# A fourth PSUM bank and another order for the seven products of the first layer

## The chip, the cores and the metric

One core of one Trainium2 chip runs the whole program. The metric is device time in microseconds (us) of one execution; lower is better. Where several executions are shown, their median is the number that counts.

## The reference, cut to what matters

Three stages follow one another: attention over 2 batches of 8 heads, 768 positions, 64 wide, with a band of 96 local and 8 global keys; a soft mixture of 8 experts over the 1536 rows that come out of it; and a second feed-forward layer with a sigmoid gate.

```python
# attention, per batch and head
a = softmax(q @ k.T / 8 + bias, masked);  x = a @ v          # x: 1536 x 512 in all
# mixture: all experts see all rows, P is made doubly balanced in 8 rounds
P = exp(x @ w_gate - max)
for _ in range(8):
    P /= P.sum(1, keepdims=True) + 1e-09
    P /= P.sum(0, keepdims=True) + 1e-09
    P *= N / E
for e in range(8):
    h = np.maximum(x @ w1[e], 0.0)       # 512 -> 1024
    out += P[:, e:e + 1] * (h @ w2[e])   # 1024 -> 512
# second feed-forward layer on that output
h = x @ w_in                             # 512 -> 2048
g = h * (1.0 / (1.0 + np.exp(-1.702 * h)))
out = g @ w_out                          # 2048 -> 512
```

## The kernel before, in words

**Steps.** The hidden width of all layers is cut into units of 256: 32 units of the experts and 8 of the second feed-forward layer. `plan` (L531) lists 80 steps, each one unit for one batch of 768 rows. A step has two halves. `layer1` (L393) makes the hidden values of the unit; `layer2` (L472) multiplies them with the second weights and adds into the output. `mixture` (L600) runs layer 1 of step n and then layer 2 of step n-1, so that hidden values have one layer 1 of time to be finished. From unit 8 on a unit is used for batch 0 and then for batch 1 in two neighbouring steps; the second of the two also splits the weights of the next unit (L667, L673). In this document **call n** is the n-th layer 1, counted from 0 to 79; in the stage that matters most the odd calls are those that split weights.

**Layer 1.** Its matrix product is done as seven half-size products in the manner of Strassen and Winograd, named by their weight operand: A11, S2, A12, S3, S1, A22, S4 (`PRODUCTS`, L60). Each product is six matmuls of 384 columns, since every operand is split into a high and a low part (three passes over two chunks). The products accumulate in three PSUM banks x, y, z (tile names pl1x, pl1y, pl1z; pool `ps_m`, three buffers):

- x holds A11, which ScalarE copies into p1 (L452), and then A11 + A12, one finished quarter of the result.
- y holds S2, then S2 + S3, then S2 + S3 + A22. VectorE reads it each time: u2 = p1 + y after S2 (L454), u3 = p1 + y after S3 (L458), p1 = p1 + y after A22 (L460). All five of these adds are recorded at L403.
- z holds S1, then S1 + S4: u3 += z after S1 (L466), u2 += z after S4 (L463).

A product that adds into a bank must wait until VectorE or ScalarE has read what stands there. `put` (L408) turns a finished quarter into the high part hh and the low part hl. For the experts that is a ReLU: in phase 3 ScalarE writes hh and VectorE hl (L430); in phase 4 only the quarter in x goes that way, and the other three take a ReLU in place (L421), a copy (L422) and a subtraction on GpSimd (L425). For the second feed-forward layer it is a gate: sigmoid on ScalarE (L415), a multiply on VectorE (L418), the high part on ScalarE (L199) and the low part on GpSimd (L205). The part called `rest` (L449) is issued after the next product.

**Layer 2.** Six row tiles of 128 (groups 0 to 5 below), each six matmuls of 512 columns into one bank (L489, tile pl), which VectorE adds into the output (L500 for the experts, L498 and L506 elsewhere) or ScalarE copies.

**Banks.** `psum` (L519) hands out the eight banks: two of kind s, two of t, one of v, three of m. Phase 1 and 2 belong to the attention, which shares the machine with the first steps. Phase 3 begins when batch 1's attention is through (L1123); there layer 2 takes its banks in the order s, s, t, v. Phase 4 begins after the expert weights P are known and applied (L1136); there the order is s, s, t, t. The next layer-2 group that gets the same bank waits until the earlier one has been read.

**Order.** Instructions are issued by this Python code in program order on each engine (L1070); nothing reorders them. Other work is mixed in by `advance` (L607): after each product and each row tile it issues a piece of the side work that is due. In phase 3 that is the preparation of batch 1's operands (L276), the logits and the balancing rounds (L320, L345) and `combine` (L383); in phase 4 it is `doubles` (L221), which turns the float64 weights of the second feed-forward layer into float32 with nine VectorE instructions (L250 to L263) in five pieces per block.

Of the kernel before, what the change touches and what calls it, by code (L numbers as in the profile page):

```python
# [7 lines left out]
F32 = mybir.dt.float32  # L8
# [7 lines left out]
P = 128  # L16
# [13 lines left out]
def f(t):  # L30
    return t.bitcast(F32)
# [16 lines left out]
class Kernel:  # L48
# [8 lines left out]

    PRODUCTS = [  # L60
        ("A11", "B11", "x"),
        ("S2", "T2", "y"),
        ("A12", "B21", "x"),
        ("S3", "T3", "y"),
        ("S1", "T1", "z"),
        ("A22", "T4", "y"),
        ("S4", "B22", "z"),
    ]
# [199 lines left out]
    def operands_open(self, b, pool, tmp):  # L268

        x = {}  # L270
        for _, nm, _ in self.PRODUCTS:
            x[nm] = tuple(pool.tile([P, 2, self.HS], F32R, tag=f"{nm}{i}", name=f"{nm}{i}_{b}") for i in "hl")
# [120 lines left out]
    def layer1(self, v, u, b, first=False):  # L393

        nc = self.nc
        HS = self.HS
        ffn = self.units[u][2] is None
        hh = self.hp.tile([P, 2, self.S], F32R, tag="hh", name=f"hh_{v}_{b}")
        hl = self.hp.tile([P, 2, self.S], F32R, tag="hl", name=f"hl_{v}_{b}")
        p1 = self.up.tile([P, HS], F32, tag="p1", name=f"p1_{v}_{b}")  # L400
        u2 = self.up.tile([P, HS], F32, tag="u2", name=f"u2_{v}_{b}")
        u3 = self.up.tile([P, HS], F32, tag="u3", name=f"u3_{v}_{b}")
        add = lambda o, x, y: nc.vector.tensor_tensor(out=o, in0=x, in1=y, op=ALU.add)  # L403
        bank = {}

        late = []

        def put(c, fc, th):  # L408


            o = slice(th * HS, th * HS + HS)
            h, l = hh[:, fc, o], hl[:, fc, o]
            if ffn:
                sg = self.sgp.tile([P, HS], F32, tag="sg", name=f"sg_{v}_{b}_{fc}_{th}")
                nc.scalar.activation(sg, c, AF.Sigmoid, scale=1.702)  # L415

                def rest():
                    nc.vector.tensor_tensor(out=sg, in0=c, in1=sg, op=ALU.mult)  # L418
                    self.split(h, l, sg)
            elif self.phase == 4 and (fc or th):  # L420
                nc.scalar.activation(c, c, AF.Relu)  # L421
                nc.scalar.activation(h, c, AF.Copy)  # L422

                def rest():
                    nc.gpsimd.tensor_tensor(out=l, in0=c, in1=f(h), op=ALU.subtract)  # L425
            else:
                nc.scalar.activation(h, c, AF.Relu)  # L427

                def rest():
                    nc.vector.scalar_tensor_tensor(out=l, in0=c, scalar=0.0, in1=f(h), op0=ALU.max, op1=ALU.subtract)  # L430
            late.append(rest)

        seen = set()

        for an, bn, k in [self.PRODUCTS[n] for n in (0, 4, 2, 1, 3, 5, 6)] if first else self.PRODUCTS:
            ah, al = self.w1[v, an]
            bh, bl = self.xops[b][bn]
            new = k not in bank
            if new:
                bank[k] = self.ps_m.tile([P, HS], F32, tag="m", name=f"pl1{k}_{v}_{b}")  # L440
            ps = bank[k]
            for i, (x, y) in enumerate([(al, bh), (ah, bl), (ah, bh)]):
                for d in range(2):

                    nc.tensor.matmul(  # L445
                        ps, x[:, d, :], y[:, d, :], start=(new and i == 0 and d == 0), stop=(i == 2 and d == 1), skip_group_check=True
                    )
            while late:
                late.pop(0)()  # L449
            seen.add(an)  # L450
            if an == "A11":
                nc.scalar.activation(p1, ps, AF.Copy)  # L452
            elif an == "S2":
                add(u2, p1, ps)  # L454
            elif an == "A12":
                put(ps, 0, 0)
            elif an == "S3":
                add(u3, p1, ps)  # L458
            elif an == "A22":
                add(p1, p1, ps)  # L460
                put(p1, 1, 0)
            elif an == "S4":
                add(u2, u2, ps)  # L463
                put(u2, 0, 1)
            if an in ("S1", "S3") and {"S1", "S3"} <= seen:
                add(u3, u3, bank["z"])  # L466
                put(u3, 1, 1)
            yield an
        late.pop(0)()
        self.h[v, b] = hh, hl  # L470
# [48 lines left out]
    def psum(self, kind, shape, name):  # L519

        if kind == "2":
            self.turnover += 1
            kinds = {2: "m", 3: "sstv", 4: "sstt"}[self.phase]
            kind = kinds[self.turnover % len(kinds)]
        elif self.phase == 1:
            kind = {"s": "m", "p": "s"}.get(kind, kind)
        kind = "t" if kind == "p" else kind
        p = {"s": self.ps_s, "t": self.ps_t, "v": self.ps_v, "m": self.ps_m}[kind]
        return p.tile(shape, F32, tag=kind, name=name)
# [52 lines left out]
    def first_weights(self, eng):  # L582
# [5 lines left out]
        yield from self.sum_weights(0)  # L588
        for an, _, _ in self.PRODUCTS:
            self.split_w1(0, an, eng)  # L590
# [628 lines left out]
```

## Time and profile before

| | |
|---|---|
| median of 3 runs | 1487.26 us (1483.48 to 1487.72) |
| the profiled execution | 1492.43 us |
| its span, first to last instruction | 1490.4 us |
| TensorE (PE) busy | 1422.0 us, 95% of the span |
| VectorE (DVE) busy | 1135.6 us, 76% |
| GpSimd (POOL) busy | 860.1 us, 58% |
| ScalarE (ACT) busy | 644.5 us, 43% |
| mean granted TensorE clock | 0.986 of full speed |

The profile is of one execution; its times are in us from the first instruction. Busy time of PE is the time in which at least one matmul was under way; matmuls overlap, so a matmul's own duration (0.33 us for 384 columns) is longer than the distance to the next one (0.17 us). A group of the waits view gives for one engine and line how long it stood idle and whose work ended that wait. Shares over the whole span mix stages that have different limits, so the stages have to be looked at one by one: attention to 243.8 us, phase 3 (calls 6 to 13) to 403.4 us, then phase 4 with the conversion of weights (calls 14 to 61) to 1178.6 us, the change to the second feed-forward layer (calls 62 to 67) to 1291.9 us, and the rest.

### The profile page before, as it was taken

The page shows a single profiled execution, that of the slowest core. Times are in us where ns is not written, and L with a number is a line of the kernel's source. Part 1 is how long each engine was busy: PE and PEld are TensorE (multiplying, and loading weights), DVE is VectorE, ACT ScalarE, POOL GpSimd, SP SyncE. Part 2 cuts the span into 40 slices and gives each one's busy share as a digit, 9 for nine tenths or more (in the row PEclk, how much of TensorE's full clock was granted, in tenths as well). Part 3 has the DMA queues.
Part 4 walks back from the last instruction along what each step waited for, and adds up shares of the span by engine and source line. Part 5 has one row for each costly group of instructions (what it writes and reads, how often), then busy time and mean ns, then how long its engine had stood idle before and what let it go on. Part 6 is the DMA issues. An engine that isn't in the chain of part 4 may idle for free.

```text
span 1490.4 us, 21158 instructions
## 1 busy us (share of the span) xinstructions
PE 1422.0 (95%) x7295; PEld 1244.4 (83%) x7295; DVE 1135.6 (76%) x2199; ACT 644.5 (43%) x1511; POOL 860.1 (58%) x1003
## 2 busy tenths in 40 slices
PE   7899998999899999999999999999999988999999
PEld 5567887788888888898888888888888877899897
DVE  7987887467578888888888888788887576555655
ACT  5676767243443333333333333333333456534332
POOL 3645555657674555554555545455555686756652
PEclk9989999999999999999999999999999999999999
DMA  5322210111221222222121212112121111101002
GB/s 147 73 61 60 73 46 29 57 57 57 75 88 62 66 73 72 71 64 68 60 75 64 82 60 72 60 61 75 61 85 47 48 38 34 52 29 43 29 1 85
DMA packets 99348, 91.66 MB, mean 61 GB/s; under 512 B 42912, under 2 KB 76704, under 8 KB 99232
## 3 DMA queue, kind: packets, MB, share of 16 engines
q1 hardware_dynamic: 99232, 90.22, 19.2%
q8 instruction: 60, 0.98, 0.3%
q14 instruction: 56, 0.46, 0.1%
HBM read 78.66 MB, written 11.53 MB: 61 GB/s over the span
## 4 chain that ended last, share of the span: by engine, by line
PE 80%; DVE 13%; issue 3%; ACT 3%; POOL 2%; POOLq 0%; DVEq 0%; ACTq 0%
PE pl L489 41%; PE pl1y L445 14%; PE pl1z L445 10%; PE pl1x L445 8%; PE pv L928 2%; DVE u L403 2%; PE s L850 1%; DVE acc L500 1%; PE pt L887 1%; DVE a L876 1%; POOL w2l L205 1%; DVE acc L285 1%; DVE a L863 1%; DVE al L908 1%; DVE hl L430 1%
## 5 line engine op out<-in xcount | busy, mean ns | idle before, releaser
L489 PE MATMUL pl<-w2h,hl 128*128 128x512 f32 x960 | 300.9, 394 | 6.9 <-DVE acc L500 4.3
L489 PE MATMUL pl<-w2l,hh 128*128 128x512 f32 x960 | 297.2, 391 | 0.0
L489 PE MATMUL pl<-w2h,hh 128*128 128x512 f32 x960 | 297.1, 391 | 0.0
L500 DVE SCALAR_TENSOR_TENSOR acc<-pl,pr,acc 128x512 f32<-128x512 f32 x312 | 230.2, 746 | 74.5 <-PE pl L489 71.9
L205 POOL TENSOR_TENSOR w2l<-r,w2h 128x512 fp32r<-128x512 f32 x100 | 131.5, 1336 | 196.7 <-ACT w2h L199 178.1
L489 PEld LDWEIGHTS pl<-w2l,hh 128*128 128x128 f32 x960 | 180.5, 188 | 39.3
L489 PEld LDWEIGHTS pl<-w2h,hh 128*128 128x128 f32 x960 | 180.4, 188 | 38.8
L489 PEld LDWEIGHTS pl<-w2h,hl 128*128 128x128 f32 x960 | 176.8, 188 | 39.8 <-DVE acc L500 5.7
L425 POOL TENSOR_TENSOR hl<-u,hh 128x384 fp32r<-128x384 f32 x100 | 105.8, 1058 | 135.1 <-ACT hh L422 134.5
L199 ACT ACTIVATE w2h<-r 128x512 fp32r<-128x512 f32 x98 | 56.6, 624 | 207.6 <-PE pl L489 174.3
L403 DVE TENSOR_TENSOR u<-p,pl1y 128x384 f32<-128x384 f32 x160 | 87.8, 549 | 64.7 <-PE pl1y L445 52.5
L452 ACT ACTIVATE p<-pl1x 128x384 f32<-128x384 f32 x80 | 39.2, 490 | 182.2 <-PE pl1x L445 167.6
L403 DVE TENSOR_TENSOR u<-u,pl1z 128x384 f32<-128x384 f32 x160 | 88.1, 551 | 36.2 <-PE pl1z L445 33.7
L421 ACT ACTIVATE u<-u 128x384 f32<-128x384 f32 x100 | 52.1, 521 | 123.6 <-DVE u L403 123.1
L205 POOL TENSOR_TENSOR hl<-sg,hh 128x384 fp32r<-128x384 f32 x64 | 66.0, 1031 | 58.1 <-ACT hh L199 56.7
L205 POOL TENSOR_TENSOR S3l<-s,S3h 128x256 fp32r<-128x256 f32 x50 | 40.5, 810 | 99.4 <-ACT S3h L199 99.2
L192 POOL TENSOR_TENSOR s<-r 128x256 f32<-128x256 f32 x100 | 78.2, 782 | 0.0
L506 DVE TENSOR_TENSOR acc<-pl,acc 128x512 f32<-128x512 f32 x84 | 54.3, 682 | 19.9 <-PE pl L489 19.8
L866 ACT ACTIVATE a<-a,m 128x288 f32<-128x288 f32 (+2 forms) x96 | 48.1, 502 | 43.0 <-DVE m L863 43.0
L445 PE MATMUL pl1y<-T3h,S3l 128*128 128x384 f32 x160 | 44.4, 358 | 23.0 <-DVE u L403 22.9
L427 ACT ACTIVATE hh<-pl1x 128x384 fp32r<-128x384 f32 x64 | 31.4, 491 | 79.5 <-PE pl1x L445 79.4
L205 POOL TENSOR_TENSOR A22l<-r,A22h 128x256 fp32r<-128x256 f32 x50 | 44.0, 880 | 22.6 <-ACT A22h L199 22.3
(259 smaller groups left out, 3489.6 us busy)
## 6 DMA issues: line engine op xcount, KB each, us to landing
r<-in_moe_w_dram SPq DMA_DIRECT2D x82, 512.0 KB, 3.6
r<-d SPq DMA_DIRECT2D x18, 512.0 KB, 3.7
d<-in_moe_w_in_dram SPq DMA_DIRECT2D x32, 256.0 KB, 2.8
d<-cx SPq DMA_DIRECT2D x64, 128.0 KB, 1.7
d<-in_moe_w_out_dram SPq DMA_DIRECT2D x32, 256.0 KB, 3.0
out_dram<-acc SPq DMA_DIRECT2D x12, 256.0 KB, 2.1
k<-in_k_dram SPq DMA_DIRECT2D x28, 96.0 KB, 2.3
q<-in_q_dram SPq DMA_DIRECT2D x28, 96.0 KB, 2.5
```

Source lines behind the costliest of these rows:

```text
L192: nc.gpsimd.tensor_tensor(out=o, in0=x, in1=y, op=op)
L199: nc.scalar.activation(hi, x, AF.Copy)
L205: e.tensor_tensor(out=lo, in0=x, in1=f(hi), op=ALU.subtract)
L403: add = lambda o, x, y: nc.vector.tensor_tensor(out=o, in0=x, in1=y, op=ALU.add)
L421: nc.scalar.activation(c, c, AF.Relu)
L425: nc.gpsimd.tensor_tensor(out=l, in0=c, in1=f(h), op=ALU.subtract)
L445: nc.tensor.matmul(ps, x[:, d, :], y[:, d, :], start=(new and i == 0 and d == 0), stop=(i == 2 and d == 1), skip_group_check=True)
L452: nc.scalar.activation(p1, ps, AF.Copy)
L489: nc.tensor.matmul(ps, x[:, c, ts_], y, start=(i == 0 and c == 0), stop=(i == 2 and c == 1))
L500: nc.vector.scalar_tensor_tensor(out=acc, in0=ps, scalar=self.pr[:, tt, e : e + 1], in1=acc, op0=ALU.mult, op1=ALU.add)
L506: nc.vector.tensor_tensor(out=acc, in0=ps, in1=acc, op=ALU.add)
L866: nc.scalar.activation(s, s, AF.Exp, bias=m, scale=-1.0, accum_out=rs[:, j : j + 1])
```

## The change

From phase 3 on layer 1 uses a table of its own, `WIDE`: the product S3 gets a fourth bank w (pool `ps_v`, tile pl1w), S3 and S1 stand ahead of A12, and A22 starts the bank y anew where it added to S2 + S3 before. The five adds become a chain: u2 = p1 + y, u3 = u2 + w, p1 = u3 + z, then u3 = u3 + y after A22 and u2 = u2 + z after S4. The quarters become finished in the order (1,1), (0,0), (1,0), (0,1), where it was (0,0), (1,1), (1,0), (0,1). In phase 3 layer 2 rotates over s, s, t, since w takes the bank of kind v. Calls 0 to 5 keep the old table, calls 6 to 79 take the new one.

```diff
--- before.py
+++ after.py
     PRODUCTS = [
         ("A11", "B11", "x"),
         ("S2", "T2", "y"),
         ("A12", "B21", "x"),
         ("S3", "T3", "y"),
         ("S1", "T1", "z"),
+        ("A22", "T4", "y"),
+        ("S4", "B22", "z"),
+    ]
+    WIDE = [
+        ("A11", "B11", "x"),
+        ("S2", "T2", "y"),
+        ("S3", "T3", "w"),
+        ("S1", "T1", "z"),
+        ("A12", "B21", "x"),
         ("A22", "T4", "y"),
         ("S4", "B22", "z"),
     ]
@@ -432,12 +442,16 @@
         seen = set()
 
-        for an, bn, k in [self.PRODUCTS[n] for n in (0, 4, 2, 1, 3, 5, 6)] if first else self.PRODUCTS:
+        wide = self.phase >= 3
+        order = self.WIDE if wide else self.PRODUCTS
+
+        for an, bn, k in [order[n] for n in (0, 4, 2, 1, 3, 5, 6)] if first else order:
             ah, al = self.w1[v, an]
             bh, bl = self.xops[b][bn]
-            new = k not in bank
-            if new:
-                bank[k] = self.ps_m.tile([P, HS], F32, tag="m", name=f"pl1{k}_{v}_{b}")
+            new = k not in bank or wide and an == "A22"
+            if k not in bank:
+                p, tag = (self.ps_v, "v") if k == "w" else (self.ps_m, "m")
+                bank[k] = p.tile([P, HS], F32, tag=tag, name=f"pl1{k}_{v}_{b}")
             ps = bank[k]
@@ -454,15 +468,24 @@
                 add(u2, p1, ps)
             elif an == "A12":
                 put(ps, 0, 0)
+            elif an == "S4":
+                add(u2, u2, ps)
+                put(u2, 0, 1)
+            elif wide:
+                if an == "S3":
+                    add(u3, u2, ps)
+                elif an == "S1":
+                    add(p1, u3, ps)
+                    put(p1, 1, 1)
+                elif an == "A22":
+                    add(u3, u3, ps)
+                    put(u3, 1, 0)
             elif an == "S3":
                 add(u3, p1, ps)
             elif an == "A22":
                 add(p1, p1, ps)
                 put(p1, 1, 0)
-            elif an == "S4":
-                add(u2, u2, ps)
-                put(u2, 0, 1)
-            if an in ("S1", "S3") and {"S1", "S3"} <= seen:
+            if not wide and an in ("S1", "S3") and {"S1", "S3"} <= seen:
                 add(u3, u3, bank["z"])
                 put(u3, 1, 1)
             yield an
@@ -520,7 +543,7 @@
-            kinds = {2: "m", 3: "sstv", 4: "sstt"}[self.phase]
+            kinds = {2: "m", 3: "sst", 4: "sstt"}[self.phase]
```

TensorE in call 17 (unit 16, batch 1; pl1x to pl1w are the banks, h and l the high and low parts), between the product S2 and the product A22, before:

```order
L445 MATMUL pl1x_16_1_25453<-B21h_1_23376,A12l_16_25171 128x384 x2
L445 MATMUL pl1x_16_1_25453<-B21l_1_23377,A12h_16_25170 128x384 x2
L445 MATMUL pl1x_16_1_25453<-B21h_1_23376,A12h_16_25170 128x384 x2
L445 MATMUL pl1y_16_1_25463<-T3h_1_23378,S3l_16_25185 128x384 x2
L445 MATMUL pl1y_16_1_25463<-T3l_1_23379,S3h_16_25184 128x384 x2
L445 MATMUL pl1y_16_1_25463<-T3h_1_23378,S3h_16_25184 128x384 x2
L445 MATMUL pl1z_16_1_25507<-T1h_1_23380,S1l_16_25201 128x384 x2
L445 MATMUL pl1z_16_1_25507<-T1l_1_23381,S1h_16_25200 128x384 x2
L445 MATMUL pl1z_16_1_25507<-T1h_1_23380,S1h_16_25200 128x384 x2
```

and with the change:

```order
L459 MATMUL pl1w_16_1_25567<-T3h_1_23457,S3l_16_25262 128x384 x2
L459 MATMUL pl1w_16_1_25567<-T3l_1_23458,S3h_16_25261 128x384 x2
L459 MATMUL pl1w_16_1_25567<-T3h_1_23457,S3h_16_25261 128x384 x2
L459 MATMUL pl1z_16_1_25579<-T1h_1_23459,S1l_16_25274 128x384 x2
L459 MATMUL pl1z_16_1_25579<-T1l_1_23460,S1h_16_25273 128x384 x2
L459 MATMUL pl1z_16_1_25579<-T1h_1_23459,S1h_16_25273 128x384 x2
L459 MATMUL pl1x_16_1_25543<-B21h_1_23455,A12l_16_25290 128x384 x2
L459 MATMUL pl1x_16_1_25543<-B21l_1_23456,A12h_16_25289 128x384 x2
L459 MATMUL pl1x_16_1_25543<-B21h_1_23455,A12h_16_25289 128x384 x2
```

A12 moved behind S3 and S1, and S3 writes a bank of its own; A11 and S2 ahead of these rows, A22 and S4 behind them stand where they stood.

VectorE in the same call (cx, cy, cz and d belong to the conversion of weights, hl is the low part of a finished quarter), from the last piece of conversion ahead of the first add to the last add, before:

```order
L261 TENSOR_SCALAR cy_3_25390<-d_2_25279 128x256
L403 TENSOR_TENSOR u2_16_1_25451<-p1_16_1_25450,pl1y_16_1_25463 128x384
L263 SCALAR_TENSOR_TENSOR cx_3_25389<-cy_3_25390,cx_3_25389 128x256
L430 SCALAR_TENSOR_TENSOR hl_16_1_25449<-pl1x_16_1_25453,hh_16_1_25448 128x384
L403 TENSOR_TENSOR u3_16_1_25452<-p1_16_1_25450,pl1y_16_1_25463 128x384
L250 TENSOR_SCALAR cx_4_25502<-d_3_25387 128x256
L251 TENSOR_SCALAR cy_4_25503<-d_3_25387 128x256
L403 TENSOR_TENSOR u3_16_1_25452<-u3_16_1_25452,pl1z_16_1_25507 128x384
L403 TENSOR_TENSOR p1_16_1_25450<-p1_16_1_25450,pl1y_16_1_25463 128x384
L253 TENSOR_TENSOR cx_4_25502<-cx_4_25502,cy_4_25503 128x256
L254 TENSOR_SCALAR cy_4_25503<-cx_4_25502 128x256
L403 TENSOR_TENSOR u2_16_1_25451<-u2_16_1_25451,pl1z_16_1_25507 128x384
```

and with the change (line numbers are those of the changed file; L413 is the add, L440 the low part of the quarter in x, L260 to L273 the conversion):

```order
L271 TENSOR_SCALAR cy_3_25480<-d_2_25368 128x256
L413 TENSOR_TENSOR u2_16_1_25541<-p1_16_1_25540,pl1y_16_1_25553 128x384
L273 SCALAR_TENSOR_TENSOR cx_3_25479<-cy_3_25480,cx_3_25479 128x256
L413 TENSOR_TENSOR u3_16_1_25542<-u2_16_1_25541,pl1w_16_1_25567 128x384
L413 TENSOR_TENSOR p1_16_1_25540<-u3_16_1_25542,pl1z_16_1_25579 128x384
L260 TENSOR_SCALAR cx_4_25595<-d_3_25477 128x256
L261 TENSOR_SCALAR cy_4_25596<-d_3_25477 128x256
L440 SCALAR_TENSOR_TENSOR hl_16_1_25539<-pl1x_16_1_25543,hh_16_1_25538 128x384
L413 TENSOR_TENSOR u3_16_1_25542<-u3_16_1_25542,pl1y_16_1_25553 128x384
L263 TENSOR_TENSOR cx_4_25595<-cx_4_25595,cy_4_25596 128x256
L264 TENSOR_SCALAR cy_4_25596<-cx_4_25595 128x256
L413 TENSOR_TENSOR u2_16_1_25541<-u2_16_1_25541,pl1z_16_1_25579 128x384
```

The number of rows is the same. The second and third add moved ahead of the low part of x, and the read of y after S3 is gone.

## Rows read from the trace of the kernel before

**Rows 1.** The page, busy time of TensorE with its share of the span.

```profile
PE 1422.0 (95%) x7295; PEld 1244.4 (83%) x7295; DVE 1135.6 (76%) x2199; ACT 644.5 (43%) x1511; POOL 860.1 (58%) x1003
```

**Rows 2.** Windows by stage: length, busy PE, PEld, DVE, ACT, POOL, clock, DMA.

```profile
243.80:403.40 159.60, 149.82 (x733) 127.27 (x732) 104.57 (x200) 65.51 (x147) 108.10 (x121) 0.98 0.17 57
403.40:1178.60 775.20, 755.67 (x3745) 674.68 (x3744) 643.87 (x1152) 276.93 (x613) 428.31 (x471) 1.00 0.21 68
```

**Rows 3.** Waits of TensorE, 403.4 to 1178.6 and 1178.6 to 1291.9: total, times, longest.

```profile
PE pl1y L445 <- DVE u L403: 18.0, 22, 2.4
PE pl1x L445 <- ACT p L452: 0.9, 1, 0.9
...
PE pl1y L445 <- DVE u L403: 1.3, 1, 1.3
```

**Rows 4.** Timeline of TensorE (start, length): first product of calls 14, 24, 25, 62.

```profile
403.41 0.51 PE L445 MATMUL pl1x<-B11h,A11l 128*128 128x384 f32 x2
...
565.08 0.51 PE L445 MATMUL pl1x<-B11h,A11l 128*128 128x384 f32 x2
...
580.59 0.51 PE L445 MATMUL pl1x<-B11h,A11l 128*128 128x384 f32 x2
...
1178.64 0.51 PE L445 MATMUL pl1x<-B11h,A11l 128*128 128x384 f32 x2
```

**Rows 5.** Timeline of TensorE in call 17: first product, and S3 with its wait.

```profile
452.05 0.51 PE L445 MATMUL pl1x<-B11h,A11l 128*128 128x384 f32 x2
...
456.17 0.61 PE L445 MATMUL pl1y<-T3h,S3l 128*128 128x384 f32 x2 [0.80 <-DVE u L403]
```

**Rows 6.** Timeline of VectorE in the same call.

```profile
452.92 1.43 DVE L259 TENSOR_TENSOR cx<-cx,cz 128x256 f32<-128x256 f32 x1
454.28 1.37 DVE L261 TENSOR_SCALAR cy<-d 128x256 int32<-128x256 int32 x1
455.57 0.54 DVE L403 TENSOR_TENSOR u<-p,pl1y 128x384 f32<-128x384 f32 x1
```

**Rows 7.** Timeline of GpSimd in the same call.

```profile
452.79 2.71 POOL L205 TENSOR_TENSOR w2l<-r,w2h 128x512 fp32r<-128x512 f32 x2 [5.91 <-ACT w2h L199]
```

**Rows 8.** One line's instructions, L259 and L403: count, shortest/median/longest in ns.

```profile
L259 DVE TENSOR_TENSOR cx<-cx,cz x64: 405/419/1433, 430.3 to 1143.0; 128x256 f32<-128x256 f32 x64
...
L403 DVE TENSOR_TENSOR u<-p,pl1y x160: 535/553/556, 113.3 to 1467.3; 128x384 f32<-128x384 f32 x160
```

**Rows 9.** Timeline of call 6 (first product at 252.05): VectorE, then S4 on TensorE.

```profile
256.59 2.58 DVE L285 TENSOR_TENSOR tmp<-xf,tmp 128x768 f32<-128x768 f32 x1
...
262.28 0.98 PE L445 MATMUL pl1z<-B22h,S4l 128*128 128x384 f32 x2 [0.72 <-DVE u L403]
```

**Rows 10.** Timeline around the layer 2 at 360.76: reads of groups 0, 2 to 5; group 3; S3 of call 12.

```profile
365.25 0.68 DVE L498 TENSOR_TENSOR accx<-pl,accx 128x512 f32<-128x512 f32 x1
...
372.35 2.47 DVE L498 TENSOR_TENSOR accx<-pl,accx 128x512 f32<-128x512 f32 x4
...
364.88 0.62 PE L489 MATMUL pl<-w2h,hl 128*128 128x512 f32 x2
...
375.43 0.59 PE L445 MATMUL pl1y<-T3h,S3l 128*128 128x384 f32 x2 [3.15 <-DVE u L403]
```

**Rows 11.** Timeline of call 78 (gate): TensorE's A11 and next layer 2, then VectorE.

```profile
1447.37 0.51 PE L445 MATMUL pl1x<-B11h,A11l 128*128 128x384 f32 x2
...
1454.70 0.63 PE L489 MATMUL pl<-w2h,hl 128*128 128x512 f32 x2
...
1452.81 0.56 DVE L403 TENSOR_TENSOR u<-u,pl1z 128x384 f32<-128x384 f32 x1 [0.48 <-PE pl1z L445]
1454.02 0.56 DVE L418 TENSOR_TENSOR sg<-u,sg 128x384 f32<-128x384 f32 x1 [0.65 <-ACT sg L415]
...
1455.69 0.96 DVE L418 TENSOR_TENSOR sg<-p,sg 128x384 f32<-128x384 f32 x1 [0.65 <-ACT sg L415]
...
1458.64 1.87 DVE L506 TENSOR_TENSOR acc<-pl,acc 128x512 f32<-128x512 f32 x3
```

## The prediction, made before the change was run

> **What bounds the kernel now.** I read the page first. TensorE is busy for 95% of the span [rows 1], so only two things can shorten the run: less matmul work, or fewer moments in which TensorE waits. The change removes no matmul, so the waits are all there is to win. The windows by stage [rows 2] say where they lie: from 403.4 to 1178.6 us TensorE works 755.7 of 775.2 us and VectorE 643.9 of 775.2, so neither is idle for long. The waits of TensorE in that stage [rows 3] are nearly all of one kind: 18.0 us in 22 waits, the longest 2.4 us, in which a product that goes into bank y waits for an add that reads y. The waits view does not show all of the loss, so I also take the distance between first and last call there. Calls 14 and 62 begin 775.23 us apart [rows 4], with 48 calls and 48 layers 2 between them. Call 24, which has no wait, takes 15.51 us up to call 25, layer 2 included [rows 4]. 48 x 15.51 = 744.5, so 30.7 us are lost in this stage: the listed waits and the slow start after each.
>
> Call 17 shows how one arises. Product S3 begins at 456.17 after a wait of 0.80 us [rows 5]. The add u2 that it waits for ran from 455.57 to 456.11, behind two instructions of the weight conversion that took 1.43 and 1.37 us [rows 6]. The first of these kinds takes 0.42 us in the median [rows 8]; here GpSimd was splitting second weights for 2.71 us at the same time [rows 7], which it does at the start of each odd call. So VectorE is late by 1 to 2 us, and between S2 and S3 stands only one product, some 1.04 us (seven products take 7.3 us), to cover it.
>
> **Term 1, calls 14 to 61.** S3 and S1 now write banks that nobody has to read first. The read of y must be done by A22, which stands three products behind S2 instead of S3's one: 2 x 1.04 = 2.1 us more cover. The longest wait was 2.4 us, so 0.3 us of it is left, and nothing of a wait of 0.8. The copy of x by ScalarE gets the same cover, so its 0.9 us goes too [rows 3]. What is late next is the read of z: S4 waits for the third add. By the order on VectorE that add follows u2 with at most a piece of conversion and u3 between. In call 17: u2 ends 456.11, conversion 0.42, u3 0.55, third add 0.55, so 457.6, that is 5.6 us after the call began at 452.05; S4's place is 6 x 1.04 = 6.3 us after it. No wait, by 0.7 us. A further blocked instruction of 1.4 us would bring one, so I leave a tenth: gain 27.6 us, bounds 0 and 30.7.
>
> **Term 2, calls 62 to 67.** One wait for u2 of 1.3 us [rows 3] and its restart: gain 1.5, bounds 0 and 3.
>
> **Term 3, phase 3.** Two places. In call 6 a subtraction of 2.58 us for batch 1's operands holds VectorE from 256.59 to 259.17, and S4 begins only at 262.28 [rows 9]. In the new order u3 and the third add follow that subtraction directly: 259.17 + 0.55 + 0.55 = 260.3, so S4 comes 2.0 us sooner. The pair of matmuls there took 0.98 us instead of some 0.51: TensorE ran at the lower of its two clock levels after standing idle; if that goes too, up to 3 us more. The price is paid in the layer 2 at 360.76. With banks s, s, t instead of s, s, t, v its group 3 takes the bank of group 0 and its group 5 that of group 2. Group 0 is read until 365.93, while group 3 now begins at 364.88; groups 2 to 5 are read from 372.35 in 0.62 us each [rows 10], and group 5 has its place at 364.88 + 2 x 1.36 = 367.6. So TensorE would stand until 373.0, 5.4 us late, and the wait of 3.15 us at S3 in call 12 that follows is then gone, since VectorE has caught up: net loss 2.2 us, up to 5 if the clock falls. The sum of both places: 0, bounds -5 and +5.
>
> **Term 4, the gates, calls 64 to 79.** TensorE has no wait to lose there, and something can be lost. The quarters pass one after another through add, sigmoid, multiply and copy, VectorE and ScalarE waiting for each other, and VectorE reads no group of layer 2 before the last multiply. In call 78 the chain starts with the add at 1452.81 and the first read of layer 2 begins at 1458.64, that is 11.27 us after the call's start at 1447.37 [rows 11]. In the new order S1 is finished one product (1.04 us) sooner, but four quarters instead of three hang in the chain; one more link costs 1455.69 - 1454.02 = 1.67 us. So that read begins 0.6 us later, at 11.9, and ends at 12.5. Group 4, which takes that bank again, has its place at 7.33 + 4 x 1.365 = 12.8 (1454.70 - 1447.37 = 7.33). 0.3 us remain. In the eight odd calls GpSimd splits weights in between, and a part of that will show: loss 2 us in all, bounds 0 and 29 (16 calls, a second link of 1.67 and half of one blocked instruction in each).
>
> Added and removed instructions: none; the adds, copies and DMAs are the same in number, and POOL's and SP's queues keep their rows but for the place of the split of S3, which now needs to be ready third. It is made a whole layer 2 (8.2 us) ahead.
>
> **Sum.** -27.6 - 1.5 + 0 + 2 = -27.1 us. Against the profiled execution 1492.43 that is 1465.3; the median of the three runs is 1487.26, 5.2 us lower, which gives 1460 for what is measured.
>
> The rule that speaks against the change stands in the Trainium skill, SBUF — State Buffer, "Who interferes with whom": a VectorE instruction with two SBUF inputs and a GpSimd instruction that reads SBUF lock each other out for a whole instruction, and only a VectorE instruction with at most one SBUF input is free of it. The trace agrees: the conversion goes from 0.42 to 1.43 us, while the adds, which read one input from PSUM, never take over 0.556 us [rows 8]. By that rule the lost time of VectorE is not removed by any order of the products, only handed on; rival A is what it would do.
>
> **Rivals.**
> A. VectorE stays late and TensorE meets it elsewhere. For: VectorE is busy for 83% of the stage [rows 2]; and in the new order the low part of the quarter in x stands behind a ReLU chain on ScalarE, so VectorE stands still where it had work. Against: it is idle for 131 us of the stage, 2.7 us per call, and TensorE's loss is only 0.64 us per call. If half of term 1 came back at S4 or in the banks of layer 2: 1460 + 13.8 = 1474.
> B. More than forecast: all of term 1, term 2 and the low-clock stretch of call 6, without the loss in phase 3: 30.7 + 1.5 + 5 = 37, so 1450.
> C. The change does not do what it says for the time: S4 takes over S3's wait one for one, because the third add comes as late after S1 as u2 came after S2. For: both are reads by the same late engine. Against: two products instead of one stand between S1 and S4. Time 1484 to 1489.
> D. Slower: the chain of the gates (term 4). Its point: the first read must end 0.3 us later than I have it before TensorE waits at all, and every further us costs 16 us. To eat up the 29 us of terms 1 and 2 it must be late by 0.3 + 29 / 16 = 2.1 us, a second extra link and a blocked multiply in every call: then 1488, and 1493 at 2.4. Against: in call 78 the multiply of 0.96 us is already the blocked kind [rows 11].
>
> **How the numbers follow.** A measurement of this kernel can tell about 0.3%, 4.5 us, from no change. Forecast (a gain of 19 to 35 us) 0.65; A 0.14; B 0.08; C 0.07; D 0.06. Faster is the forecast, A and B: 0.87; same is C: 0.07; slower is D: 0.06. The range takes in the forecast with the bounds of term 3 and A: 1449 to 1476.
>
> **What would show it.** Right: the waits of pl1y for u2 between calls 14 and 61 fall from 18.0 us to under 3, the 48 calls with their layers 2 take about 747 us instead of 775, and a new wait of layer 2 for VectorE of some 5 us stands near 365 us in place of the 3.15 us at S3. Wrong: waits of pl1z for the adds of more than 10 us (A, C), waits of layer 2 for VectorE in the last 200 us (D), or a distance of calls above 15.5 us with no wait in it.

## The result and the profile after

| | kernel before | changed |
|---|---|---|
| median, runs on one chip | 1487.49 us (1483.48 to 1489.29, 4 runs) | 1464.34 us (1460.04 to 1465.24, 4 runs) |
| ratio, 95% interval | | 0.9842 (0.9814 to 0.9870) |
| profiled execution, its span | 1492.43, 1490.4 us | 1460.04, 1457.7 us |

The change is faster by 23 us, 1.6%; forecast were 1460 us and a range of 1449 to 1476. The page of the changed kernel, the line that answers to [rows 1]:

```profile
PE 1404.6 (96%) x7295; PEld 1238.7 (85%) x7295; DVE 1116.5 (77%) x2199; ACT 642.1 (44%) x1511; POOL 860.1 (59%) x1003
```

Every engine has as many instructions as before. TensorE is 17.4 us less busy with the same matmuls: 9.0 us less in calls 14 to 61 (746.7 instead of 755.7), and 6.0 us less before call 0 (74.6 instead of 80.6), where both kernels run the same code. In calls 14 to 61 part of this belongs to the waits: a pair of matmuls behind a stand, a moment in which TensorE waits, counts as busy for longer (0.61 us instead of 0.51, [rows 5]).

The windows by stage of the changed kernel (columns as in [rows 2]: length, busy PE, PEld, DVE, ACT, POOL, clock, DMA), calls 14 to 61, then calls 6 to 13 (the first line of [rows 2] begins earlier, at the start of phase 3):

```profile
398.50:1146.10 747.60, 746.66 (x3745) 674.79 (x3744) 629.45 (x1152) 277.26 (x613) 429.41 (x471) 1.00 0.22 70
245.50:398.50 153.00, 140.73 (x696) 119.70 (x696) 97.83 (x194) 58.33 (x134) 101.20 (x116) 0.99 0.17 56
```

In the stage of calls 14 to 61 VectorE does its 1152 instructions in 629 us, 14 us less than before, but in 27.6 us less time, and TensorE is idle for 0.9 us of 747.6. Its waits there, which answer to [rows 3] (waited for: total, times, longest), and the first products of calls 14 and 62, which answer to [rows 4]:

```profile
PE pl1z L459 <- DVE p L413: 0.4, 2, 0.3
PE pl1y L459 <- DVE u L413: 0.3, 1, 0.3
```

```profile
398.53 0.51 PE L459 MATMUL pl1x<-B11h,A11l 128*128 128x384 f32 x2
...
1146.11 0.51 PE L459 MATMUL pl1x<-B11h,A11l 128*128 128x384 f32 x2
```

The 48 calls with their layers 2 take 1146.11 - 398.53 = 747.58 us, where they took 775.23.

One profile against one profile says little of the stages that the change does not touch, so both kernels were profiled once more (runs e7 and e8 below). From the first products of calls 0, 6, 14, 62, 68 and the spans:

| us | before | before again | changed | changed again |
|---|---|---|---|---|
| start to call 0 | 98.5 | 94.3 | 90.6 | 90.7 |
| calls 0 to 5 | 153.5 | 154.8 | 154.9 | 154.9 |
| calls 6 to 13 (phase 3) | 151.4 | 151.4 | 153.0 | 153.0 |
| calls 14 to 61 | 775.2 | 773.4 | 747.6 | 747.6 |
| calls 62 to 67 | 113.2 | 112.3 | 113.1 | 115.8 |
| call 68 to the end | 198.5 | 198.6 | 198.5 | 198.6 |
| span | 1490.4 | 1484.9 | 1457.7 | 1460.5 |

The first pair differs by 32.7 us, the second by 24.4, the medians by 23. What the first pair has too much lies for the most part before call 0, where both kernels run the same code. Another 1.6 us of it lie in call 47 of the kernel before: behind its longest stand (2.36 us at S3) TensorE was granted the lower of its two clock levels (0.50 from 940.8 to 944.1), and the call took 19.72 us. In the second profile the same call, at the full clock, took 18.14.

Call 17 of the changed kernel shows how the gain comes about (VectorE, then GpSimd, then TensorE's S3 and S4):

```profile
445.92 1.45 DVE L269 TENSOR_TENSOR cx<-cx,cz 128x256 f32<-128x256 f32 x1
447.28 1.38 DVE L271 TENSOR_SCALAR cy<-d 128x256 int32<-128x256 int32 x1
448.59 0.54 DVE L413 TENSOR_TENSOR u<-p,pl1y 128x384 f32<-128x384 f32 x1
...
450.11 0.55 DVE L413 TENSOR_TENSOR p<-u,pl1z 128x384 f32<-128x384 f32 x1
```

```profile
445.78 2.73 POOL L215 TENSOR_TENSOR w2l<-r,w2h 128x512 fp32r<-128x512 f32 x2 [4.73 <-ACT w2h L209]
```

```profile
447.15 0.51 PE L459 MATMUL pl1w<-T3h,S3l 128*128 128x384 f32 x2
...
451.31 0.51 PE L459 MATMUL pl1z<-B22h,S4l 128*128 128x384 f32 x2
```

VectorE is held up exactly as before: 1.45 and 1.38 us for the two pieces of conversion, against 1.43 and 1.37 [rows 6], beside the same split on GpSimd. u2 begins at 448.59, 3.54 us after the call's start; before it was 3.52. But S3, which waited 0.80 us for it [rows 5], now begins at its place at 447.15, 1.44 us ahead of u2. The third add ends at 450.66 and S4 has its place at 451.31: 0.65 us to spare, where the prediction had 0.7. Not every odd call has so much. In seven of the 24 S4 begins 0.05 us after the third add ends, so it waited for it, in five of them by too little to be listed (call 19 is shown at e9).

### The profile page after: what moved, and what is told of

Same layout as the page of the kernel before. It is cut to its first block, busy times and chain, and to the rows that moved or that the text cites. A ratio compares the mean times of both kernels' runs of the same rounds, so it can differ in the third digit from the quotient of the medians.

```text
span 1457.7 us, 21271 instructions
## 1 busy us (share of the span) xinstructions
PE 1404.6 (96%) x7295; PEld 1238.7 (85%) x7295; DVE 1116.5 (77%) x2199; ACT 642.1 (44%) x1511; POOL 860.1 (59%) x1003
## 4 chain that ended last, share of the span: by engine, by line
PE 69%; DVE 3%; ACT 1%; issue 1%; POOL 1%; DVEq 0%; ACTq 0%
PE pl L512 37%; PE pl1z L459 9%; PE pl1x L459 9%; PE pl1y L459 9%; PE pl1w L459 5%; DVE acc L295 1%; DVE sg L428 0%; DVE acc L523 0%; DVE u L413 0%; ACT sg L425 0%; PE pr L539 0%; DVE p L413 0%; POOL s L202 0%; ACT hh L209 0%; POOL hl L215 0%
## 5 line engine op out<-in xcount | busy, mean ns | idle before, releaser
L523 DVE SCALAR_TENSOR_TENSOR acc<-pl,pr,acc 128x512 f32<-128x512 f32 x312 | 226.9, 744 | 54.6 <-PE pl L512 53.1
L435 POOL TENSOR_TENSOR hl<-p,hh 128x384 fp32r<-128x384 f32 x50 | 51.5, 1031 | 85.6 <-ACT hh L432 85.6
L431 ACT ACTIVATE p<-p 128x384 f32<-128x384 f32 x50 | 26.3, 526 | 157.8 <-DVE p L413 157.8
L413 DVE TENSOR_TENSOR u<-p,pl1y 128x384 f32<-128x384 f32 x86 | 47.2, 549 | 55.0 <-PE pl1y L459 45.0
L440 DVE SCALAR_TENSOR_TENSOR hl<-pl1x,hh 128x384 fp32r<-128x384 f32 x64 | 35.6, 556 | 58.0 <-ACT hh L437 57.7
L431 ACT ACTIVATE u<-u 128x384 f32<-128x384 f32 x100 | 52.0, 520 | 54.6 <-DVE u L413 54.3
```

Of the source, the lines that this page charges most:

```text
L523: nc.vector.scalar_tensor_tensor(out=acc, in0=ps, scalar=self.pr[:, tt, e : e + 1], in1=acc, op0=ALU.mult, op1=ALU.add)
```

## The experiments

Eleven runs were made in three batches (e1 to e4, e5 to e8, e9 to e11), each batch on one chip beside the kernel before; ratios are to it. **Cover**, in the expectations and below, is the number of products between the one whose result is read and the next write of that bank. Line numbers of a variant can be some lines off from those of the kernel it was made from.

### The two halves of the change, each alone

**e2, the bank without the order.** The table `WIDE` keeps the old sequence, S3 has its own bank:

```diff
     WIDE = [
         ("A11", "B11", "x"),
         ("S2", "T2", "y"),
+        ("A12", "B21", "x"),
         ("S3", "T3", "w"),
         ("S1", "T1", "z"),
-        ("A12", "B21", "x"),
         ("A22", "T4", "y"),
```

> The fourth bank without the new order: A11, S2, A12, S3 (into w), S1, A22, S4. Cover theory: S3 never waits and A22 has three products of cover, but only A22 (1.04 us) stands between S1 and S4, so the third add, which comes behind the lateness of the odd calls, is waited for at S4: 0.3 to 1 us in most odd calls of 14 to 61, the stage at 755 to 765 us, the whole 8 to 17 us longer than with the change (1472 to 1481). Rival (the bank is all that matters, the order nothing): the stage within 2 us of 747.6 and the whole as with the change.

Measured: 1478.87 us (6 runs), ratio 0.9945 (0.9925 to 0.9965). Calls 14 to 61 took 765.8 us, just above what was expected, and the longest wait was 1.5 us instead of 1. The waits of TensorE there:

```profile
PE pl1z L459 <- DVE p L413: 13.4, 22, 1.5
...
PE pl1y L459 <- DVE u L413: 0.3, 1, 0.3
```

The wait for y is all but gone (A22 now stands three products behind the last product that the read of y waits for, S2), but the wait for z has taken its place: between S1 and S4 stands one product. This is what rivals A and C of the prediction described, and it is what the other half of the change prevents.

**e3, the order without the bank.** From the kernel before, with S1 and A12 ahead of S3; S3 and A22 both still add into y (the table is used from phase 3 on; that line of the edit is left out here):

```diff
+    WIDE = [
+        ("A11", "B11", "x"),
+        ("S2", "T2", "y"),
+        ("S1", "T1", "z"),
+        ("A12", "B21", "x"),
+        ("S3", "T3", "y"),
+        ("A22", "T4", "y"),
+        ("S4", "B22", "z"),
+    ]
...
```

> The new place of S1 without the fourth bank: A11, S2, S1, A12, S3, A22, S4 in banks x, y, z as before, layer 2 in phase 3 with s, s, t, v. Cover theory: S3 has two products of cover now and waits in few calls, but A22 follows S3 into the same bank with nothing between, so it waits for the read of y in every call: 0.2 us until VectorE starts, 0.55 us for the add, 0.06 us to start again, some 0.8 us x 74 calls = 60 us, against 27 us won at S3: 1515 to 1525, with 48 waits or more of pl1y in calls 14 to 61. Rival (what counts is VectorE's total lateness, not the distance between two products of one bank): as before, 1480 to 1490.

Measured: 1535.64 us (4 runs), ratio 1.0324 (1.0299 to 1.0349). The sign was right and the size too small: the rise is 49.5 us. Calls 14 to 61 took 806.7 us, with this wait in every one of the 48:

```profile
PE pl1y L455 <- DVE u L413: 45.3, 48, 2.0
```

With no product between S3 and A22 even a VectorE that is in time costs TensorE a stand in each call, 0.94 us on the mean (45.3 / 48): the whole add of 0.55 us and what passes before and behind it. The same wait stands in the gates' calls (calls 68 to 78: 181.2 us instead of 171.0), which the expectation had left out.

### What makes VectorE late

**e6, the kernel before without GpSimd's split of second weights:**

```diff
     for c in range(FW // P) if only is None else [only]:
         h = self.wp.tile([P, 512], F32R, tag=f"w2h{c}", name=f"w2h{c}_{v}")
+        if self.phase == 4 and self.units[self.versions[v]][2] is not None:
+            l = self.w2[v - 1, c][1]
+            self.nc.scalar.activation(h, r2[:, c, :], AF.Copy)
+        else:
...
```

> The kernel before, but in phase 4 GpSimd does not make the low part of the experts' second weights: the low part of an earlier unit is used instead, so the output is another. Some 48 GpSimd instructions of 1.29 us at the start of the odd calls are gone, VectorE's instructions all stay. Lock theory (VectorE is late because GpSimd's split holds it up): the conversion ahead of u2 takes 0.42 us instead of 1.43, waits of S3 for u2 fall from 18.0 us to under 6, calls 14 to 61 take 750 to 760 us, time 1461 to 1473. Rival (VectorE is late by its own load of 83%): waits of 12 us or more, calls 14 to 61 over 768 us, time 1480 to 1489.

Measured: 1463.97 us (4 runs), ratio 0.9833 (0.9818 to 0.9848), as fast as the change, with three banks and the old order (it leaves out the low part of these weights). The stage of calls 14 to 61 took 750.7 us, 3.1 more than in the change. Its window, its one wait of TensorE, and VectorE in call 17 (the two pieces of conversion and u2):

```profile
405.56:1156.23 750.67, 748.99 (x3746) 674.19 (x3745) 595.93 (x1152) 276.89 (x614) 360.83 (x421) 1.00 0.21 70
```

```profile
PE pl1x L449 <- ACT p L456: 0.9, 1, 0.9
```

```profile
454.19 0.41 DVE L263 TENSOR_TENSOR cx<-cx,cz 128x256 f32<-128x256 f32 x1
454.52 0.29 DVE L265 TENSOR_SCALAR cy<-d 128x256 int32<-128x256 int32 x1
455.72 0.56 DVE L407 TENSOR_TENSOR u<-p,pl1y 128x384 f32<-128x384 f32 x1 [0.92 <-PE pl1y L449]
```

VectorE has the same 1152 instructions and needs 595.9 us for them instead of 643.9 [rows 2]. Without the split it is ahead of TensorE: u2 stands 0.92 us and waits for S2. So the lateness is not VectorE's load of 83%, it is the hold-up by GpSimd, and 50 GpSimd instructions (471 - 421) cost VectorE 48 us. The rival falls.

**e5, the kernel before with the conversion behind u2.** After the last row tile of layer 2 and after A11 no piece is issued; it is caught up after S2:

```diff
...
-                advance()
+                if k == "A11" and side and side[0][0] == "doubles":
+                    debt[0] += side[0][2]
+                else:
+                    advance()
```

> The kernel before, three banks and the old order; only the piece of weight conversion that stood between the last row tile of layer 2 and the add u2 is issued behind u2. Cover theory (a late VectorE meets TensorE wherever a read has one product of cover): u2 is in time, but the two blocked instructions now stand ahead of u3, which reads y for A22 with one product of cover; by the rows of call 17 u3 would end some 1.2 us after A22's place. The wait moves from S3 to A22, calls 14 to 61 take 765 to 776 us, the time is 1476 to 1488. Rival (the place of the conversion was the fault, no bank is needed): waits of the stage under 5 us, calls 14 to 61 in 755 us or less, time 1468 or less.

Measured: 1494.01 us (5 runs), ratio 1.0039 (1.0026 to 1.0052): slower by 0.4%, where 1476 to 1488 us were expected. Calls 14 to 61 took 782.8 us, 7 more than the cover theory's upper end. The waits of the stage, then call 17 on VectorE (u2, conversion, u3) and A22 on TensorE:

```profile
PE pl1y L445 <- DVE u L403: 25.4, 24, 2.1
```

```profile
445.62 0.56 DVE L403 TENSOR_TENSOR u<-p,pl1y 128x384 f32<-128x384 f32 x1 [1.45 <-PE pl1y L445]
446.09 0.68 DVE L259 TENSOR_TENSOR cx<-cx,cz 128x256 f32<-128x256 f32 x1
446.69 0.83 DVE L261 TENSOR_SCALAR cy<-d 128x256 int32<-128x256 int32 x1
...
448.85 0.54 DVE L403 TENSOR_TENSOR u<-p,pl1y 128x384 f32<-128x384 f32 x1
```

```profile
449.44 0.62 PE L445 MATMUL pl1y<-T4h,A22l 128*128 128x384 f32 x2 [0.81 <-DVE u L403]
```

u2 now waits for TensorE (1.45 us), S3 stands no longer, and A22 stands instead, 0.81 us for u3. The side work fills the place behind u2 and there it meets the next read with one product of cover. Moving the work without more cover only moves the wait.

### How much the cover carries

**e9 and e10, the split done twice over,** in the change and in the kernel before:

```diff
             self.split(h, l, r2[:, c, :], eng)
+            if self.phase == 4 and self.units[self.versions[v]][2] is not None:
+                self.nc.gpsimd.tensor_tensor(out=l, in0=r2[:, c, :], in1=f(h), op=ALU.subtract)
```

> The change, with GpSimd making the low part of the experts' second weights twice over in phase 4: 5.4 us at the start of each odd call instead of 2.7, the result the same. Cover theory: VectorE is held up for twice as long; the margin of S4 was worked out as 0.7 us, so the two products of cover are used up now and waits of 0.5 to 1.5 us appear at S4 or A22 in most odd calls: calls 14 to 61 take 755 to 775 us, time 1472 to 1492, and the rise (8 to 28 us) is smaller than that of the kernel before with the same doubling. Rival (the order has room to spare): calls 14 to 61 stay under 750 us, time 1467 or less.

> The kernel before with the same doubling. Cover theory: with one product of cover behind every read each further us of hold-up shows: besides the 18 us at S3 there are waits at A22 for u3 as in the run with the conversion behind u2 (25 us); calls 14 to 61 take 795 to 815 us, time 1507 to 1527. Rival (the hold-up is over by then, since VectorE has idle time behind u2): within 5 us of the kernel before.

Measured: e9 1482.32 us (10 runs), ratio 0.9966 (0.9951 to 0.9980); e10 1512.05 us (4 runs), ratio 1.0171 (1.0149 to 1.0192). Calls 14 to 61 took 763.4 and 797.1 us, 15.8 and 21.9 more than without the doubling. The times and lengths are within what the cover theory had put down, and the change loses less by the doubling (18.0 us) than the kernel before (24.6). The waits of e10 are smaller than expected: 31.5 us for S3 and A22 together, where 18 and some 25 were put down. The waits of the stage, of the change with the doubling and of the kernel before with it:

```profile
PE pl1z L461 <- DVE p L415: 11.3, 14, 1.5
PE pl1y L461 <- DVE u L415: 1.8, 2, 1.5
```

```profile
PE pl1y L447 <- DVE u L405: 31.5, 33, 3.5
PE pl1z L447 <- DVE u L405: 3.3, 7, 0.5
```

The margin is small. In call 19 of the change the third add ends at 482.36 and S4 begins at 482.42, 0.1 us behind its place, so there is none left; in call 19 of e9 S4 waits 1.10 us. The third add and S4 in the change, then S4 in e9:

```profile
481.81 0.55 DVE L413 TENSOR_TENSOR p<-u,pl1z 128x384 f32<-128x384 f32 x1
482.42 0.62 PE L459 MATMUL pl1z<-B22h,S4l 128*128 128x384 f32 x2
...
489.77 0.62 PE L461 MATMUL pl1z<-B22h,S4l 128*128 128x384 f32 x2 [1.10 <-DVE p L415]
```

e10 shows the single hold-ups plainly, here in call 19, GpSimd and then VectorE:

```profile
481.97 1.29 POOL L205 TENSOR_TENSOR w2l<-r,w2h 128x512 fp32r<-128x512 f32 x1 [5.82 <-ACT w2h L199]
483.34 1.29 POOL L220 TENSOR_TENSOR w2l<-r,w2h 128x512 fp32r<-128x512 f32 x1
484.58 1.46 POOL L205 TENSOR_TENSOR w2l<-r,w2h 128x512 fp32r<-128x512 f32 x1
```

```profile
482.15 1.25 DVE L258 TENSOR_SCALAR cz<-d 128x256 int32<-128x256 int32 x1
483.44 1.46 DVE L259 SCALAR_TENSOR_TENSOR cz<-cz,cy 128x256 f32<-128x256 int32 x1
484.83 0.54 DVE L405 TENSOR_TENSOR u<-p,pl1y 128x384 f32<-128x384 f32 x1
```

A conversion instruction that starts beside a GpSimd instruction ends 0.1 to 0.3 us after that one has ended; the add u2, with one input in PSUM, takes its usual 0.54 us beside the third GpSimd instruction.

### Phase 3

**e1, the change in phase 4 alone** (`wide = self.phase == 4`, and the rotation s, s, t, v kept):

> The new table from phase 4 on only; phase 3 (calls 6 to 13) keeps the three-bank table and its layer 2 keeps s, s, t, v. Cover theory (a wait is as long as VectorE's lateness minus the products that stand between a read and the next write): calls 14 to 61 keep their 747.6 us, calls 6 to 13 go back from 153.0 us to the 151.4 us of before, the layer 2 near 360 us has no wait of 1.5 and 3.7 us, and the wait of about 3 us at S3 in call 12 is back. So the whole is 1 to 2 us shorter than with the change. Rival (the change gained in phase 3 too, and the start of the run hides it): 2 to 4 us longer than with the change.

Measured: 1463.39 us (5 runs), ratio 0.9832 (0.9808 to 0.9856). Phase 3 took 151.6 us, calls 14 to 61 took 747.5: the whole gain of the change is phase 4's, and what it does in phase 3, the order and the rotation s, s, t together, loses 1.4 us by the stage, too little for the runs to tell.

**e4 and e11, the change with s, s, t, t in phase 3,** the same kernel in two batches:

```diff
-            kinds = {2: "m", 3: "sst", 4: "sstt"}[self.phase]
+            kinds = {2: "m", 3: "sstt", 4: "sstt"}[self.phase]
```

> The change, with layer 2 taking four banks s, s, t, t in phase 3 too. Cover theory: the waits of 1.5 and 3.7 us in the layer 2 near 360 us go, about 1 us comes back in call 12 at A22, and the balancing rounds, which use the t banks, meet layer 2 a little more often: the whole 2 to 5 us shorter than with the change. Rival (the t banks are held by the logits and rounds, so layer 2 waits there instead): same as the change or up to 4 us longer.

> The change with layer 2 over s, s, t, t in phase 3, in more rounds. Phase 3 was 2.85 us shorter by the trace than in the change: a ratio of 0.981 to 0.983, below the change's 0.9844 (0.9831 to 0.9858).

> The change, unchanged, in more rounds, to be set beside the variant with layer 2 over s, s, t, t in phase 3 (ratio 0.9819, 0.9797 to 0.9841). If that rotation costs what the trace says (5.4 us of waits less the wait of 3.2 that is gone, some 2 to 3 us of phase 3), the ratio here is 0.9835 to 0.985; if it costs nothing, 0.982.

Measured: e4 1460.75 us (5 runs), ratio 0.9819 (0.9797 to 0.9841); e11 1462.39 us (5 runs), 0.9831 (0.9812 to 0.9850); the change again, e8, 1464.03 us (5 runs), 0.9844 (0.9831 to 0.9858). By their intervals the two kernels are not told apart. By the stage they are: phase 3 took 150.1 and 150.2 us in the two profiles of the variant, 153.0 in both of the change. Where the rotation s, s, t costs it, in the layer 2 at 351.75 of the changed kernel (its groups 3 and 5), and the waits of layer 2 for the same reads in phase 3 of e4:

```profile
357.52 0.73 PE L512 MATMUL pl<-w2h,hl 128*128 128x512 f32 x2 [1.49 <-DVE accx L521]
...
364.26 0.73 PE L512 MATMUL pl<-w2h,hl 128*128 128x512 f32 x2 [3.71 <-DVE accx L521]
```

```profile
PE pl L512 <- DVE accx L521: 1.3, 3, 0.9
```

So the change with layer 2 keeping four banks in phase 3 is the shortest by the stages; that it is faster than the change is not shown by the runs.

**e7, the kernel before for a second profile:**

> The kernel before, unchanged, for a second profile. If the late start of the first one (first product of call 0 at 98.5 us, the five later profiles have 90.4 to 93.7) was of that execution, it stands at 90 to 94 here and the span is 1482 to 1486; if it belongs to the kernel before, at 98 again. Calls 14 to 61 take 775 us within 1 in both cases.

Measured: 1486.86 us (1 run), span 1484.9, first product of call 0 at 94.3 us, calls 14 to 61 in 773.4 (1.8 us less than in the first profile, where 1 was allowed), with the same waits for u2 of 18.0 us in 22. The span is within the expected 1482 to 1486 and the start just above the expected 94, so the first profile's late start does not belong to the kernel. Of the 1.8 us 1.6 are call 47 with its clock.

## Why the prediction was right, and where it was not

**What bounds it, and term 1: right.** Predicted -27.6 us for calls 14 to 61 and "about 747" for their length; measured -27.6 and -25.9 in the two pairs of profiles, and 747.6. That the first is exact is luck, since 1.6 us of it are call 47's clock. Predicted under 3 us of waits for u2; measured 0.3, in call 47, whose wait of 2.4 us was the one of which the prediction left 0.3. The margin of 0.7 us at S4, read from call 17, does not hold in every odd call; where it is gone, the listed waits come to 0.4 us in all. The cause that was read from one call (VectorE held up by GpSimd's split, one product of cover) is what e6 and e5 show for the stage: take the split away and the wait is gone without the change; move the conversion and the wait moves. The table puts the runs in order of cover.

| run | reads that wait | cover | waits, calls 14 to 61 | length |
|---|---|---|---|---|
| e3 | u3 of y, ahead of A22 | 0 | 45.3 us in 48 | 806.7 |
| before | u2 of y, ahead of S3 | 1 | 18.0 in 22 | 775.2 |
| e2 | third add of z, ahead of S4 | 1 | 13.4 in 22 | 765.8 |
| changed | both | 3 and 2 | 0.7 in 3 | 747.6 |
| e6, no split | u2 of y, ahead of S3 | 1 | none for VectorE | 750.7 |

The loss is larger than the listed waits in each row; in the kernel before 775.2 - 744.5 = 30.7 us against 18.0 + 0.9 + 0.5 = 19.4. In call 17 a wait listed with 0.80 us costs 1.1: S3 begins at 456.17, 0.97 us behind its place (A12 begins at 454.16 and takes 1.04), since a wait is counted only from the end of the matmul before it, and S3 then takes 1.17 us, up to the start of S1 at 457.34, instead of 1.04. The prediction put all of the 30.7 us down to the listed waits and the slow start after each; 1.6 us of it are call 47's clock.

**Rival A: its mechanism came, its cost did not.** VectorE stands behind the ReLU chain of the quarter in x, as A said. VectorE's waits in the stage, of the kernel before and of the change:

```profile
DVE acc L500 <- PE pl L489: 61.0, 119, 0.8
...
DVE hl L430 <- ACT hh L427: 10.0, 21, 1.4
```

```profile
DVE hl L440 <- ACT hh L437: 54.6, 48, 1.8
DVE acc L523 <- PE pl L512: 41.9, 88, 0.8
```

It stands 54.6 us there instead of 10.0, once in every call, and makes it up from its idle time elsewhere: TensorE waits for nothing in it.

**The hold-up.** In e10 a held-up instruction ends 0.1 to 0.3 us after GpSimd's, and in e6, without the split, VectorE needs 48 us less. By the Trainium skill, SBUF — State Buffer, "Who interferes with whom", the two engines lock each other out for a whole instruction where both want the shared ports. The runs agree: 1.43 and 1.37 us beside the split [rows 6], 0.41 and 0.29 without it. The prediction told the rule too short, so that it reads as if any instruction with one SBUF input were free of it, but the 1.37 us are of a `TENSOR_SCALAR` that reads `d` alone. The same section of the Trainium skill counts `tensor_scalar` among the operations that can take the shared ports, when its operands meet certain conditions. What rival A drew from it, that the lost time is handed on and not removed, holds for VectorE (629 of 644 us are still there) and not for TensorE.

**Term 2: wrong.** "One wait for u2 of 1.3 us and its restart: gain 1.5, bounds 0 and 3." The two pairs give a gain of 0.2 and a loss of 3.5 us. The wait of 1.3 us for u2 is gone, but others are longer: all waits that the view lists there come to some 10.5 and 9.4 us before and to 11.6 in both profiles of the change. Calls 62 to 67, the kernel before (second profile), then the change (second profile):

```profile
PE pl L489 <- DVE acc L500: 4.3, 4, 3.2
PE pl L489 <- ACT acc L504: 2.5, 1, 2.5
PE pl1y L445 <- DVE u L403: 1.3, 1, 1.3
```

```profile
PE pl L512 <- ACT acc L527: 4.1, 2, 3.6
PE pr L539 <- DVE acc L523: 3.2, 1, 3.2
PE pl L512 <- DVE acc L523: 3.2, 3, 2.4
```

Here a call that is through sooner waits in the layer 2 behind it: in the first profiles call 64 fell from 10.5 to 8.4 us and the layer 2 after it rose from 11.9 to 14.0, in the second profiles from 10.1 to 7.3 and from 10.9 to 16.3. The step that failed is that the wait was taken as lost time without asking what the next product would then wait for. Why the two pairs disagree is in the clock that TensorE was granted in calls 62 to 67:

| | before | before again | changed | changed again |
|---|---|---|---|---|
| calls 62 to 67, us | 113.2 | 112.3 | 113.1 | 115.8 |
| mean granted clock there | 0.98 | 0.98 | 1.00 | 0.97 |
| stretches at 0.50 | 1217.2 to 1220.6 | 1212.2 to 1215.6 | none | 1201.3 to 1204.7, 1225.1 to 1228.6 |

Each of these stretches begins at most 1.5 us after the end of a stand of 3.2 to 3.6 us, but in the first profile of the change the clock stayed full behind stands of 3.1 and 3.6. TensorE is busy in them at half its clock, so each costs some 1.7 us, half its length (an estimate). Without them the stage would take 111.5 and 113.1 us in the first pair, 110.5 and 112.4 in the second. By the same reckoning e1 and e4, which run the change's code here, come to 110.4 and 110.3 us (115.5 and 115.4 with three such stretches each), no more than the kernel before. So neither pair shows the gain of 1.5 us; whether the change gains or loses a microsecond here is open.

**Term 3: right in its places, a little too good.** Predicted 0, with bounds of -5 and +5; measured a loss of 1.6 and 1.5 us. The price came as described: 1.49 + 3.71 = 5.2 us of new waits (5.4 predicted), and the 3.15 us at S3 [rows 10] are gone; calls 11 and 12 with their layers 2 took 35.9 us in the first profile before and 38.5 in the change, 2.6 more (2.2 predicted). Behind the stand of 3.71 us the clock fell to 0.51 from 365.2 to 368.7, which the prediction had allowed for. The rotation as a whole costs 153.0 - 150.2 = 2.8 us against s, s, t, t. Call 6 gave less: S4 came sooner,

```profile
253.94 0.59 PE L459 MATMUL pl1z<-B22h,S4l 128*128 128x384 f32 x2 [1.97 <-DVE p L413]
```

8.4 us after the call's start instead of 10.2, 1.8 of the 2.0 predicted. But the layer 2 behind it then waits for GpSimd's split of second weights (1.4 us) and for VectorE (1.3 us), neither of which it did before. Call 6 with its layer 2 took 24.95 us in the first profile before, with the clock at 0.50 from 261.5 to 268.3 behind its waits, 22.25 in the second, at the full clock, and 23.9 in both of the change. So the low clock in call 6, which the prediction counted as a possible gain, does not come in every execution; in the second profile before it stands in call 12 instead (0.51 from 369.1 to 376.0). In e4 and e11 the clock is full throughout phase 3, which is then only 1.2 us shorter than before.

**Term 4: no loss.** Predicted 2 us, bounds 0 and 29. TensorE has no wait behind call 68, as before, and the time from there to the end is 198.5 in both. In call 78 (TensorE's first product, VectorE's first read of layer 2):

```profile
1414.37 0.51 PE L459 MATMUL pl1x<-B11h,A11l 128*128 128x384 f32 x2
...
1426.11 3.30 DVE L529 TENSOR_TENSOR acc<-pl,acc 128x512 f32<-128x512 f32 x5
```

The read begins 11.74 us after the call's start; 11.9 was predicted and 11.27 it was [rows 11]. So rival D's mechanism came as sized in call 78, and no call has a wait of TensorE that would show its point (a first read that ends later than 12.8) to be reached.

**The sum.** Terms 1 to 4 were -27.1 us. By the stages the first pair of profiles gives -27.6 - 0.2 + 1.6 + 0 = -26.2, the second -25.9 + 3.5 + 1.5 + 0 = -20.9, and the medians differ by 23.2. So the forecast of 1460 was 4 us too low: term 2's gain did not come, phase 3 cost 1.5 us, and the 2 us that term 4 did not cost stand against them. Errors of either sign met in the sum.

## What to carry to other kernels

Where TensorE waits for a read of its bank, count the products between the one that is read and the next write of that bank, for every bank and in microseconds, and set that against the worst hold-up of the reading engine: here 1.04 us were too few, 2.1 just enough and 3.1 enough in all calls but one for a hold-up of 2.7 us. A bank alone moves the wait to the next pair with little cover, an order alone can make it worse; side work that is moved out of the way of one read lands in front of the next. And look for who holds the reader up: removing that, if it can be removed, was worth as much here as the bank and the order together.

## What the hardware showed beyond that

The time before call 0, in which all kernels run the same code, differs from one execution to the next by up to 9.5 us, for the most part with the mean clock that TensorE was granted there. Windows from the start to the first product of call 0, of the kernel before and of e5 (columns as above; the clock stands third from the end):

```profile
0.00:98.52 98.52, 80.63 (x473) 58.73 (x473) 82.03 (x259) 62.90 (x186) 52.26 (x100) 0.90 0.40 99
```

```profile
0.00:89.05 89.05, 70.70 (x472) 51.29 (x472) 78.33 (x254) 60.17 (x182) 50.97 (x97) 0.98 0.44 109
```

At a mean of 0.98 of the full 2.4 GHz it takes 89 us, at 0.90 it takes 98, and e6, one of the faster kernels, has one of the late starts (98.2 us at 0.90). The mean clock alone does not settle it: e9 took 94.4 us at 0.89. Why an execution gets the one or the other was not tried. Two profiles of different kernels can so differ by 9 us without any cause in the kernels; comparing stages, and a second profile of each, takes that out.
